# Moving the down-projection weights to other buffers at a stage boundary of a fused forward-and-backward kernel

## The chip, the cores and the metric

The kernel runs on one core of a Trainium2 chip. The metric is the device time of one execution in microseconds (us). The kernel before took 2054.99 us as the median of five runs (2052.01 to 2065.15). One further execution was taken by the hardware profiler.

The engines that appear below are PE (TensorE, the matrix unit; PEld is its weight load), DVE (VectorE), ACT (ScalarE), POOL (GpSimd) and SP (SyncE, which here only issues DMAs). SP, ACT and POOL each issue DMAs into a queue of their own; "SPq" in a profile line is the issue itself. An engine works through its own instructions in program order, so an instruction that waits holds back everything behind it on that engine.

## The reference

The program computes a block and all its gradients for a sequence of S = 2048 tokens, D = 1024 channels and F = 3584 hidden channels:

```
xn  = layernorm(x)
s   = xn * (longconv(shiftconv(k) * v) + ssm_D * shiftconv(k) * v)   # sequence mixing, by FFT
h   = (xn @ w_gate) * (xn @ w_up)                                    # [S, F]
g   = silu(h @ w_down)                                               # [S, D]
out = x + s * g
```

and then, for a given `grad_out`, the gradients for x, k, v, shift_k, ssm_k, ssm_D, w_gate, w_up and w_down. All inputs and outputs are bf16.

## The kernel before, in words

The work is laid out in stages for PE, and other engines' work is woven between them. Tokens come in 16 blocks of 128 (`b`), hidden channels in 14 slabs of 256 (`sl`) or 28 blocks of 128 (`fc`).

1. **Gate and up projection.** For each slab and each group of four token blocks, `gu_unit` does 32 matmuls (L556). ACT copies each PSUM result into `gut` (L558), and ACT stores `gut` to DRAM as `GUd`. DVE multiplies the halves into `hN`, and POOL stores that as `Hd`. A deferred closure `turn` transposes `hN` on PE (L570), ACT copies the result to `hT` (L571, two buffers) and POOL stores it as `HTd`. The forward convolution (PE, DVE, ACT) is pumped in between; its result goes out over POOL as `YFd`. The last two slabs (12 and 13) run together: first for the token blocks 0 to 7 (`hf = 0`), then for 8 to 15 (`hf = 1`).
2. **Down projection.** For each token block `b`, `bm_mm` (L967) does 28 x 2 matmuls with `w_down` into one PSUM tile `psbm` of three. The blocks go in pairs `bp`; the transposed `h` of a pair is `ht`, loaded from `HTd` (`load_ht`, two buffers). For the first pair it is `HT0`, in the two buffers U4 and U5. The first pair's matmuls run with `fc` outermost, four matmuls for each `fc`. After each block, `gate` loads four rows from DRAM (`x_t`, `do_t`, `xn_t`, `yf_t`), and ACT and DVE make the output and the gradients that flow back from the gate; they are stored by POOL as `DBMd`, `DYd` and `DXNAd`.
3. **Gradients of h, gate and up weights.** `dh_half` (L1091) and `dw_slab` (L1110), with the backward convolution pumped in between on DVE, PE, ACT and POOL.
4. **Gradient of the down weights** (L1209), then **gradient of x** (L1232).

**The buffers.** Eight tiles U0 to U7, of 1 MB each (128 partitions x 4096 bf16), live from the start. U0 to U3 hold the transposed normalised input `XNT` in stage 1, four token blocks each, so the last to read U0 and U1 are the matmuls of slab 13 in `hf = 0`, and the last to read U2 and U3 those of slab 13 in `hf = 1`. Four more, U8 to U11 (pool `ub`), and the `ht` buffers (pool `mh`) are allocated only after stage 1, in the memory that stage 1's pools (`fw`, `fg`: the slabs, `gut`, `hN`, `hT`) leave, so the first load into them waits until stage 1's last store of these has landed.

`WD[j]` are the seven 1 MB pieces of `w_down` that stage 2 reads, four `fc` each. Before, WD0 and WD1 are in U6 and U7 and are loaded before the last two slabs; WD2 and WD3 are in U2 and U3, WD4 to WD6 in U9, U10 and U8, and they are loaded after stage 1. `DBMT` (stage 2 and 3, transposed gradient of the gate) is in U0, U1, U4 and U5; `XN` (the normalised input for stage 3) in U7 to U10; `gu_in` cycles `GUd` pieces through U11, U6, U2, U3 and U12.

**The order.** The program text gives each instruction its place; a scheduler then orders each engine's instructions. It hoists loads: the eight gate rows of blocks 0 and 1 are written after the matmuls in the text, but stand in SP's order between the loads of WD2 and WD4. `tc.issue_after(x)` keeps what stands under it behind `x`. SP's order around the boundary, before:

```
WD0, WD1, HT0[0], HT0[1] rows 16-23, HT0[1] rows 24-27,
WD2 (U2), x_t do_t xn_t yf_t (block 0), WD3 (U3), x_t do_t xn_t yf_t (block 1),
WD4 (U9), WD5 (U10), WD6 (U8), ht of pair 1, ht of pair 2, ...
```

The loads under `ld` all have line L62 and the stores under `st` line L65, as each is issued by a helper.

Of the kernel before, what the change touches and what calls it, by code (L numbers as in the profile page):

```python
# [19 lines left out]
def build_kernel(  # L20
# [17 lines left out]
    DC = D // P  # L38
# [22 lines left out]
    def ld(out, in_):  # L61
        return nc.sync.dma_start(out=out, in_=in_)  # L62

    def st(out, in_):
        return nc.gpsimd.dma_start(out=out, in_=in_)  # L65
# [15 lines left out]
    def pool(name, bufs=1, side=None, space=None):  # L81
        kw = dict(name=name, bufs=bufs, reuse_waits="tile")
        if side:
            kw["side"] = side
        if space is not None:
            kw["space"] = space
        return tc.alloc_tile_pool(**kw)
# [109 lines left out]
    def tt(o, a, b, op):  # L197
        V.tensor_tensor(o, a, b, op)  # L198
# [261 lines left out]
    def u8(i, pat="p (a x) -> p a x", **kw):  # L460
        return U[i][:].rearrange(pat, **kw)
# [76 lines left out]
    def defer(fn):  # L538
        later.append([0, fn])

    def flush(age=0):

        for e in later:
            e[0] += 1
        while later and later[0][0] >= age:
            later.pop(0)[1]()
# [194 lines left out]
    def load_wd(j):  # L741
        return ld(WD[j], B_w_down[j * 512:(j + 1) * 512, :].rearrange("(c p) d -> p c d", p=P))

    def ht_rows(bp, f0, f1):
        j = (bp % 4) * 256
        return HTd[bp // 4][f0 // 24][f0 % 24 * P:(f0 % 24 + f1 - f0) * P, j:j + 256].rearrange("(c f) s -> f c s", f=P)


    WD = [u8(6, a=4), u8(7, a=4)]
    HT0 = [u8(4, a=16), u8(5, a=16)]  # L750
    with tc.issue_after(slab_ld.ins):
        load_wd(0)
# [2 lines left out]
    for hf in range(2):  # L755
        if hf == 1:
            flush()
            ld(HT0[1][:, 8:12], ht_rows(0, 24, 28))
        for sl in range(NSL - 2, NSL):
            for b0 in (8 * hf, 8 * hf + 4):  # L760
                gu_unit(sl, b0, 4, slabs[sl - NSL + 2], tick)
            if (hf, sl) == (0, NSL - 2):

                assert len(h_out) == 8
                ld(HT0[1][:, 0:8], ht_rows(0, 16, 24))
# [193 lines left out]
    bpump, bdrain = make_pump(conv_backward(), C_TOTAL)  # L959

    ddo = const.tile([P, 8], BF16, name="ddo")
    WD += [u8(j, a=4) for j in (2, 3, 9, 10, 8)]
    DBMT = [u8(q, a=DC) for q in (0, 1, 4, 5)]

    def bm_mm(ps, ht, i, fc):
        for dh in range(2):
            nc.tensor.matmul(ps[:, dh * 512:(dh + 1) * 512], ht(fc)[:, i * P:(i + 1) * P],  # L967
                             WD[fc // 4][:, fc % 4, dh * 512:(dh + 1) * 512], start=(fc == 0), stop=(fc == NF - 1))

    tr_name = ["tr"]  # L970

    def gate(b, ps):
        c, r = divmod(b, 8)
        ins = []
        for nm_, src in (("x_t", xq[:, c, r, :]), ("do_t", gout[:, c, r, :]), ("xn_t", XNd[:, b, :]), ("yf_t", YFd[:, b, :])):
            t = mi.tile([P, D], BF16, name=nm_)
            ld(t[:], src)
            ins.append(t[:])
        x_t, do_t, xn_t, yf_t = ins
        T = lambda nm_: mt.tile([P, D], BF16, name=nm_)[:]  # L980
        O = lambda nm_: mo.tile([P, D], BF16, name=nm_)[:]
        bm, sig, sgn, gg, so, dgg, ds_t = [T(n_) for n_ in ("bm", "sig", "sgn", "gg", "so", "dgg", "ds_t")]
        dbm, dy, dxa, o_t = [O(n_) for n_ in ("dbm", "dy", "dxa", "o_t")]
        nc.scalar.copy(out=bm, in_=ps[:])
        nc.scalar.activation(sig, bm, ACT.Sigmoid)
        nc.scalar.activation(sgn, bm, ACT.Sigmoid, scale=-1.0)
        tt(so, xn_t, yf_t, MUL)
        tt(dgg, do_t, so, MUL)
        tt(gg, bm, sig, MUL)
        tt(sgn, sgn, gg, MUL)  # L990
        tt(sig, sig, sgn, ADD)
        tt(dbm, dgg, sig, MUL)
        st(DBMd[b * P:(b + 1) * P, :], dbm)
        tt(ds_t, do_t, gg, MUL)
        tt(dy, ds_t, xn_t, MUL)
        st(DYd[:, :, b, :].rearrange("e u d -> u e d"), dy.rearrange("u (e d) -> u e d", e=8))
        tt(dxa, ds_t, yf_t, MUL)
        st(DXNAd[:, b, :], dxa)
        tt(o_t, so, gg, MUL)
        tt(o_t, o_t, x_t, ADD)  # L1000
        st(o_out[:, c, r, :], o_t)

        def turn():
            ps = ps_tr.tile([P, DC, P], BF16, name=tr_name[0])
            for dc in range(DC):
                nc.tensor.transpose(ps[:, dc, :], dbm[:, dc * P:(dc + 1) * P], ident[:])
            nc.scalar.copy(out=DBMT[b // 4][:, :, (b % 4) * P:(b % 4 + 1) * P], in_=ps[:])
        if b >= 12:
            defer(turn)
# [18 lines left out]
            ld(t, GUd[k // 2, k % 2])  # L1028
            DGU[k] = t

    for j in range(2, 7):
        wd_ld = load_wd(j)
    with tc.issue_after(wd_ld.ins):
        ht1 = load_ht(1)
# [4 lines left out]
    for i in range(2):  # L1039
        gate(i, pss[i])  # L1040
    for bp in range(1, 8):
        ht, ht_ld = load_ht(bp) if bp > 1 else ht1
        if bp in (3, 5, 7):
            q = (bp - 3) // 2
            with tc.issue_after(ht_ld.ins):
                nc.sync.dma_start_transpose(out=DBMT[q], in_=DBMd[512 * q:512 * q + 512, :])
        if bp == 6:
# [13 lines left out]

    XN = [u8(q, a=4) for q in (7, 8, 9, 10)]
    bg = pool("bg", 2, side="right")
    U.append(bg.tile([P, 4096], BF16, name="U12", bufs=1))
    ps_b = ps_tr = pool("ps_b", 3, space=PSUM)
# [7 lines left out]
    def btick(n):  # L1075
        bcnt[0] += n
        bpump((bcnt[0] - 10) / (BT - 10))

    def dh_half(k, wdt):
# [3 lines left out]
        for g in range(2):  # L1083
            bs = slice(4 * g, 4 * g + 4)
            dht = bg.tile([P, 4, SLW], BF16, name="dht", bufs=3)
            for e in range(2):
                ps = ps_b.tile([P, 512], F32, name="psb")
                for x in range(2):
                    b = 4 * g + 2 * e + x
                    for dc in range(DC):  # L1090
                        nc.tensor.matmul(ps[:, x * SLW:(x + 1) * SLW], DBMT[2 * hf + g][:, dc, (b % 4) * P:(b % 4 + 1) * P],  # L1091
                                         wdt[:, dc, :], start=(dc == 0), stop=(dc == DC - 1))
# [13 lines left out]
    def dw_slab(sl, dgus):  # L1106
        for dc in range(DC):
            ps = ps_b.tile([P, 512], F32, name="psb")
            for b in range(NB):
                nc.tensor.matmul(ps[:], XN[b // 4][:, b % 4, dc * P:(dc + 1) * P],  # L1110
                                 dgus[b // 8][:, b % 8].rearrange("p a f -> p (a f)"),
# [9 lines left out]
    def load_h(sl, home):  # L1121
        h = u8(home, "p (b f) -> p b f", b=NB)
        ld(h, Hd[sl])
        return h
# [6 lines left out]
    for q in range(4):  # L1131
        ld(XN[q], XNd[:, 4 * q:4 * q + 4, :])
    for k in (3, 4):
        gu_in(k)
    first = dh_half(0, wdt)
    DBM = [u8(q, a=4) for q in (0, 1, 4, 5)]
    HSL = (3, 11, 6)
    for sl in range(NSL):
        dgus = [first, dh_half(2 * sl + 1, wdts[sl])]
# [4 lines left out]
        else:  # L1144

            hs = {0: load_h(0, HSL[0])}
            for q in range(4):
                ld(DBM[q], DBMd[512 * q:512 * q + 512, :].rearrange("(b u) d -> u b d", u=P))
            hs[1] = load_h(1, HSL[1])
# [14 lines left out]
    def load_wgu(n, store):  # L1164
        a, j = pieces[n]
        WGU[n] = store
        nc.sync.dma_start_transpose(out=store, in_=(B_w_gate, B_w_up)[a][:, j * 512:(j + 1) * 512])

    def load_dgut(g, n):

        a, j = pieces[n]
        t = (gd2 if n < 4 else gd).tile([P, 4, 512], BF16, name=f"dgut{n}")
        nc.sync.dma_start_transpose(out=t[:], in_=DGd[j, a, 512 * g:512 * g + 512, :])
        return t
# [3 lines left out]
    for k in range(NSL):  # L1178
        if 0 < k and k + 1 < NSL:
            hs[k + 1] = load_h(k + 1, HSL[(k + 1) % 3])  # L1180
        if k == 0:
            hs[2] = load_h(2, HSL[2])
        with tc.issue_after(wst.ins) if k > 0 else nullcontext():
            if k in (1, 2, 3, 4, 5):
                load_wgu(k - 1, u8((7, 8, 9, 10, 2)[k - 1], a=4))
            if k in (6, 7, 8, 9):
                ts.append(load_dgut(0, k - 6))
        if k == 11:

            bdrain()  # L1190
            tip.release()
            gw = pool("gw", 1)
            gd = pool("gd", 1)
            for i in range(2):
                load_wgu(5 + i, gw.tile([P, 4, D], BF16, name=f"W{i}")[:])
            ts += [load_dgut(0, n) for n in range(4, 7)]
        if k == 12:
            load_wgu(7, u8(6, a=4))
            ts.append(load_dgut(0, 7))
        if k == 13:  # L1200
            load_wgu(8, u8(3, a=4))
            ts.append(load_dgut(0, 8))
        h = hs.pop(k)
        for f in range(2):
            wbs = wo.tile([P, D], BF16, name="wbs")[:]
            for dh in range(2):
                ps = ps_b.tile([P, 512], F32, name="psb")
                for b in range(NB):
                    nc.tensor.matmul(ps[:], h[:, b, f * P:(f + 1) * P], DBM[b // 4][:, b % 4, dh * 512:(dh + 1) * 512],  # L1209
                                     start=(b == 0), stop=(b == NB - 1))  # L1210
                nc.scalar.copy(out=wbs[:, dh * 512:(dh + 1) * 512], in_=ps[:])  # L1211
                btick(2)
            f0 = k * SLW + f * P
            wst = ld(o_dwd[f0:f0 + P, :], wbs)
# [50 lines left out]
            V.scalar_tensor_tensor(dx_t[:, cl], dxn[:, cl], RSTD[:, b:b + 1], dout_t[:, cl], op0=MUL, op1=ADD)  # L1265
            (st if parts == 1 else ld)(o_dx[:, c, r, cl], dx_t[:, cl])

    for i, j in enumerate((11, 0, 1, 4, 5)):
        load_wgu(9 + i, u8(j, a=4))
        ts.append(load_dgut(0, 9 + i))  # L1270
    for g in range(4):
# [88 lines left out]
```

## Time and profile before

| what | value |
|---|---|
| median of five runs | 2054.99 us (2052.01, 2052.61, 2054.99, 2063.32, 2065.15) |
| the profiled execution, device time | 2053.47 us |
| its span, first to last instruction | 2051.7 us, so 1.8 us lie around the span |
| PE busy | 1970.5 us, 96% of the span |
| DVE busy | 1485.3 us, 72% |
| ACT busy | 607.3 us, 30% |
| POOL busy | 343.7 us, 17% |
| DMA moved | 454.43 MB, mean 221 GB/s |
| stage 2, PE (L967) | from 572.1 to 774.4 us |

A line of the timeline reads: start in us, duration in us, engine, source line, operation, output <- inputs, shape, how many instructions were merged, and in brackets how long the engine had been idle before and what ended that. "PE busy" counts matmuls from issue to modelled end, so it says little about how fast the matmuls run; the distance between their starts does. PEclk is the clock that PE was granted, 1.00 being full. A line of the waits gives who waited, for whom, for how long in all, how many times, and the longest.

### The profile page before, as it was taken

How to read it: one execution, taken by the hardware profiler on the slowest of the kernel's cores; microseconds unless marked ns; L12 is line 12 of the kernel's file. 1: busy time of each engine (PE TensorE's matmuls, PEld its weight loads, DVE VectorE, ACT ScalarE, POOL GpSimd, SP SyncE). 2: the span in 40 equal slices, each digit the busy share in tenths (PEclk: the TensorE clock that was granted, in tenths of full speed). 3: DMA queues.
4: the chain of work that ended last, by engine and by line, in shares of the span. 5: the costliest groups of instructions: out<-in, count | busy, mean ns of one | idle time of the engine just before them, and what ended most of it. 6: DMA issues, size and time to landing. Idle time of an engine off the chain costs nothing.

```text
span 2051.7 us, 28854 instructions
## 1 busy us (share of the span) xinstructions
PE 1970.5 (96%) x11530; PEld 1056.2 (51%) x11530; DVE 1485.3 (72%) x2007; ACT 607.3 (30%) x956; POOL 343.7 (17%) x499
## 2 busy tenths in 40 slices
PE   6999999999989998999899889999999999999998
PEld 3455555555534445666566556555444444444443
DVE  7789999999826654888799999998978024444343
ACT  4644444445422223232222222222122101111112
POOL 4222222221112221000112211211111100110100
PEclk9999999999999999999999999999999999999999
DMA  9686766558499989675878688865996979393921
GB/s 300 226 281 218 247 211 237 195 195 277 171 306 303 273 273 317 209 220 164 273 247 262 223 229 242 263 219 197 253 233 174 241 186 213 115 215 93 235 69 57
DMA packets 468711, 454.43 MB, mean 221 GB/s; under 512 B 249456, under 2 KB 393624, under 8 KB 454624
## 3 DMA queue, kind: packets, MB, share of 16 engines
q1 hardware_dynamic: 324240, 190.08, 36.1%
q0 software_dynamic: 45200, 189.08, 27.3%
q10 hardware_dynamic: 99136, 73.42, 11.4%
q8 instruction: 90, 1.47, 0.3%
q14 instruction: 45, 0.37, 0.1%
HBM read 208.15 MB, written 194.02 MB: 196 GB/s over the span
## 4 chain that ended last, share of the span: by engine, by line
PE 60%; DVE 16%; issue 14%; DMA 5%; POOL 3%; ACT 1%; ACTq 0%; POOLq 0%; DVEq 0%; SPq 0%
PE psx L1232 19%; PE psb L1110 10%; PE psb L1209 9%; PE psbm L967 9%; DVE W L198 5%; PE psg L556 4%; DVE m L198 4%; PE psb L1091 4%; DVE HX L198 1%; DVE U L198 1%; DMA dyl<-DYd 1%; DVE KX L198 1%; POOL HTd L65 1%; PE psdk L943 1%; DVE B L242 1%
## 5 line engine op out<-in xcount | busy, mean ns | idle before, releaser
L556 PE MATMUL psg<-wslab,U 128*128 128x512 bf16 x1792 | 419.0, 385 | 8.0 <-DMA wslab<-in_B_w_gate_dram 3.1
L1110 PE MATMUL psb<-U,U 128*128 128x512 bf16 x1792 | 399.3, 382 | 10.5 <-ACT dht L1093 6.5
L1232 PE MATMUL psx<-U,dgut 128*128 128x512 bf16 x1536 | 335.7, 379 | 0.0
L1110 PEld LDWEIGHTS <-U 128*128 128x128 bf16 x1792 | 176.1, 98 | 215.3 <-issue 16.8
L1232 PEld LDWEIGHTS <-dgut 128*128 128x128 bf16 x1792 | 173.9, 98 | 211.0 <-issue 3.6
L556 PEld LDWEIGHTS <-U 128*128 128x128 bf16 x1792 | 174.8, 99 | 197.8 <-issue 16.9
L1091 PE MATMUL psb<-wdt,U 128*128 128x256 bf16 x1792 | 204.0, 274 | 10.1 <-ACT dht L1093 8.9
L558 ACT CAST gut<-psg 128x512 bf16<-128x512 f32 x224 | 131.3, 587 | 230.6 <-PE psg L556 219.5
L1209 PE MATMUL psb<-U,U 128*128 128x512 bf16 x896 | 195.8, 379 | 0.0
L1091 PEld LDWEIGHTS <-U 128*128 128x128 bf16 x1792 | 175.8, 98 | 33.9 <-issue 10.7
L967 PE MATMUL psbm<-U,ht 128*128 128x512 bf16 x784 | 169.9, 379 | 0.0
L1114 ACT CAST wb<-psb 128x512 bf16<-128x512 f32 x112 | 65.6, 586 | 313.5 <-PE psb L1110 217.5
L198 DVE TENSOR_TENSOR W<-W 128x1024 f32<-128x1024 f32 (+1 forms) x144 | 142.6, 1008 | 2.8
L1209 PEld LDWEIGHTS <-U 128*128 128x128 bf16 x896 | 87.1, 98 | 102.4
L198 DVE TENSOR_TENSOR m<-A,B 128x1024 bf16<-128x1024 bf16 (+1 forms) x160 | 116.5, 791 | 29.7 <-issue 21.1
L198 DVE TENSOR_TENSOR dka<-dkh,Wbc 128x1024 bf16<-128x1024 bf16 x16 | 11.1, 692 | 165.0 <-DMA dkh<-DKSHd 165.0
L967 PEld LDWEIGHTS <-ht 128*128 128x128 bf16 x784 | 76.6, 98 | 91.8
L1255 ACT ACTIVATE dx_t<-dxn 128x1024 bf16<-128x1024 f32 (+1 forms) x17 | 17.1, 1007 | 341.1 <-DVE dxn L198 287.1
L1093 ACT CAST dht<-psb 128x512 bf16<-128x512 f32 x112 | 65.0, 587 | 156.4 <-PE psb L1091 109.8
L198 DVE TENSOR_TENSOR U<-U,dht 128x2048 bf16<-128x2048 bf16 x56 | 70.2, 1254 | 25.1 <-ACT dht L1093 25.1
L198 DVE TENSOR_TENSOR W<-W,psP 128x512 f32<-128x512 f32 x128 | 80.4, 678 | 8.6 <-ACT W L228 6.7
L1211 ACT CAST wbs<-psb 128x512 bf16<-128x512 f32 x56 | 32.8, 586 | 159.5 <-PE psb L1209 145.3
(233 smaller groups left out, 2339.9 us busy)
## 6 DMA issues: line engine op xcount, KB each, us to landing
U<-GUd SPq DMA_DIRECT2D x28, 1024.0 KB, 7.5
DGd<-U ACTq DMA_DIRECT2D x56, 512.0 KB, 6.0
GUd<-gut ACTq DMA_DIRECT2D x54, 512.0 KB, 4.5
A<-DYFd POOLq DMA_DIRECT2D x16, 1024.0 KB, 5.5
U<-Hd SPq DMA_DIRECT2D x15, 1024.0 KB, 6.0
out_dram<-wb ACTq DMA_DIRECT2D x224, 64.0 KB, 3.7
Hd<-hN POOLq DMA_DIRECT2D x54, 256.0 KB, 3.5
HTd<-hT POOLq DMA_DIRECT2D x54, 256.0 KB, 3.7
```

Source lines behind the costliest of these rows:

```text
L65: return nc.gpsimd.dma_start(out=out, in_=in_)
L198: V.tensor_tensor(o, a, b, op)
L556: gu_mm[0] = nc.tensor.matmul(ps[:], XNT[q][:, dc, qi * P:(qi + 1) * P], w[:, dc].rearrange("p a f -> p (a f)"), start=(dc == 0), stop=(dc ...
L558: nc.scalar.copy(out=gut[:, i].rearrange("p a f -> p (a f)"), in_=ps[:])
L967: nc.tensor.matmul(ps[:, dh * 512:(dh + 1) * 512], ht(fc)[:, i * P:(i + 1) * P], WD[fc // 4][:, fc % 4, dh * 512:(dh + 1) * 512], start=(f ...
L1091: nc.tensor.matmul(ps[:, x * SLW:(x + 1) * SLW], DBMT[2 * hf + g][:, dc, (b % 4) * P:(b % 4 + 1) * P], wdt[:, dc, :], start=(dc == 0), sto ...
L1093: nc.scalar.copy(out=dht[:, 2 * e:2 * e + 2].rearrange("p b f -> p (b f)"), in_=ps[:])
L1110: nc.tensor.matmul(ps[:], XN[b // 4][:, b % 4, dc * P:(dc + 1) * P], dgus[b // 8][:, b % 8].rearrange("p a f -> p (a f)"), start=(b == 0), ...
L1114: nc.scalar.copy(out=wb[:].rearrange("p a f -> p (a f)"), in_=ps[:])
L1209: nc.tensor.matmul(ps[:], h[:, b, f * P:(f + 1) * P], DBM[b // 4][:, b % 4, dh * 512:(dh + 1) * 512], start=(b == 0), stop=(b == NB - 1))
L1211: nc.scalar.copy(out=wbs[:, dh * 512:(dh + 1) * 512], in_=ps[:])
L1232: nc.tensor.matmul(ps[:, dh * 512:(dh + 1) * 512], t[n][:, f, i * P:(i + 1) * P], WGU[n][:, f, dh * 512:(dh + 1) * 512], start=(n == 0 and ...
```

## The change

The changed kernel gives five of the seven pieces of `w_down` other buffers, loads two of them earlier in the text, and puts the gate rows of the first two blocks behind the last of them.

- WD2 and WD3 go to U0 and U1, WD4 and WD5 to U2 and U3, and WD6 to U9. WD2 and WD3 are loaded in the text at the start of `hf = 1`, ahead of the last HT0 rows.
- `DBMT` and later `DBM` go to U10, U8, U4 and U5 in place of U0, U1, U4 and U5. `XN` goes to U7, U0, U1 and U9 in place of U7 to U10. The homes of the transposed gate and up weights in stage 4 follow.
- The loads of the gate rows of blocks 0 and 1 stand under `issue_after(wd_ld.ins)`, where `wd_ld` is the load of WD6.

```diff
-    WD = [u8(6, a=4), u8(7, a=4)]
+    WD = [u8(j, a=4) for j in (6, 7, 0, 1)]
...
         if hf == 1:
             flush()
+            load_wd(2)
+            wd_ld = load_wd(3)
             ld(HT0[1][:, 8:12], ht_rows(0, 24, 28))
...
-    WD += [u8(j, a=4) for j in (2, 3, 9, 10, 8)]
-    DBMT = [u8(q, a=DC) for q in (0, 1, 4, 5)]
+    WD += [u8(j, a=4) for j in (2, 3, 9)]
+    DBMT = [u8(q, a=DC) for q in (10, 8, 4, 5)]
...
             t = mi.tile([P, D], BF16, name=nm_)
-            ld(t[:], src)
+            with tc.issue_after(wd_ld.ins) if b < 2 else nullcontext():
+                ld(t[:], src)
...
-    for j in range(2, 7):
+    for j in range(4, 7):
         wd_ld = load_wd(j)
...
-    XN = [u8(q, a=4) for q in (7, 8, 9, 10)]
+    XN = [u8(q, a=4) for q in (7, 0, 1, 9)]
...
-    DBM = [u8(q, a=4) for q in (0, 1, 4, 5)]
+    DBM = [u8(q, a=4) for q in (10, 8, 4, 5)]
...
-                load_wgu(k - 1, u8((7, 8, 9, 10, 2)[k - 1], a=4))
+                load_wgu(k - 1, u8((7, 0, 1, 9, 2)[k - 1], a=4))
...
-    for i, j in enumerate((11, 0, 1, 4, 5)):
+    for i, j in enumerate((11, 10, 8, 4, 5)):
```

The order in which PE, DVE, ACT and POOL run their instructions is the same in both kernels. SP's order around the boundary, after:

```
WD0, WD1, HT0[0], HT0[1] rows 16-23,
WD2 (U0), WD3 (U1), HT0[1] rows 24-27, WD4 (U2), WD5 (U3), WD6 (U9),
ht of pair 1, x_t do_t xn_t yf_t (block 0), x_t do_t xn_t yf_t (block 1), ht of pair 2, ...
```

At the end of stage 2, SP's order was GU1, XN, GU2, XN, XN, XN, GU3, GU4 (1 MB each) and becomes GU1, XN, XN, GU2, XN, XN, GU3, GU4. Nothing else in SP's order differs but the names of the buffers.

## The prediction

> **What bounds the kernel now.** First the page's first part: PE is busy for 1970.5 of 2051.7 us, so only a stage in which PE stands still can give time. Then PE's waits in the stretch of stage 2's first pair, and its timeline there.
>
> ```profile
> PE 1970.5 (96%) x11530; PEld 1056.2 (51%) x11530; DVE 1485.3 (72%) x2007; ACT 607.3 (30%) x956; POOL 343.7 (17%) x499
> ```
>
> ```profile
> PE psbm L967 <- DMA U<-in_B_w_down_dram: 5.7, 2, 5.4
> ```
>
> ```profile
> 572.09 10.52 PE L967 MATMUL psbm<-U,U 128*128 128x512 bf16 x48
> 582.92 3.61 PE L967 MATMUL psbm<-U,U 128*128 128x512 bf16 x16 [0.31 <-DMA U<-in_B_w_down_dram]
> 591.89 12.00 PE L967 MATMUL psbm<-U,U 128*128 128x512 bf16 x48 [5.35 <-DMA U<-in_B_w_down_dram]
> 603.72 16.57 PE L967 MATMUL psbm<-U,ht 128*128 128x512 bf16 x76
> ```
>
> PE stops twice for `w_down`: before its fourth piece (WD3, after 48 matmuls) and its fifth (WD4, after 64). The first row gives the pace: (10.52 - 0.38) / 47 = 0.216 us from start to start. At that pace the 112 matmuls of the pair end at 572.09 + 112 x 0.2158 = 596.26, and the next pair begins at 603.72. So 7.46 us are lost: 0.47 at WD3, 5.52 at WD4, and 1.47 in the row after it, whose 48 matmuls took 11.83 us where 10.36 would do.
>
> Why WD4 is late is read in the chain of work, SP's timeline and ACT's.
>
> ```profile
> 580.43 5.70 DMA HTd<-hT
> ...
> 586.35 5.50 DMA U<-in_B_w_down_dram
> ```
>
> ```profile
> 562.77 0.37 SPq L62 DMA_DIRECT2D U<-in_B_w_down_dram  x1
> 563.28 0.41 SPq L62 DMA_DIRECT2D x_t<-in_A_q_dram  x1
> 563.74 0.43 SPq L62 DMA_DIRECT2D do_t<-in_grad_out_dram  x1
> 564.21 0.66 SPq L62 DMA_DIRECT2D xn_t<-XNd  x1
> 574.56 0.33 SPq L62 DMA_DIRECT2D yf_t<-YFd  x1
> 574.99 0.42 SPq L62 DMA_DIRECT2D U<-in_B_w_down_dram  x1
> ...
> 586.35 1.48 SPq L62 DMA_DIRECT2D U<-in_B_w_down_dram  x3
> 587.87 18.50 SPq L62 DMA_DIRECT2D ht<-HTd  x4
> ```
>
> ```profile
> 579.13 1.01 ACT L571 COPY hT<-tr 128x1024 bf16<-128x1024 bf16 x1 [7.54 <-DMA HTd<-hT]
> ```
>
> WD3's buffer is free at 570.1 (the last gate-and-up matmul), but SP sits on `yf_t`, which waits until the store of `YFd` (issued at 564.02) has landed, and issues WD3 at 574.99. WD4 to WD6 wait for the last `HTd` store: the third `hT` copy needs a buffer whose store landed at 579.1; so that store was issued at 580.43, landed at 586.13, and SP issued WD4 at 586.35.
>
> **What the Trainium skill says.** "DMA: Bandwidth & Descriptors", section "Anatomy of one DMA — SWDGE (gpsimd) path": a wait is made by the issuing engine before it dispatches, so one waiting load holds all behind it. The trace agrees: `yf_t` held WD3 for 4.5 us. The same page, "Queues, rings and completion order": the 16 DMA engines take turns between the queues that have work, and serve one queue in order. The trace fits: with WD2 and three gate rows on SP's queue, `YFd` needed 10.5 us, and 8.4 us at 517 us with fewer loads. "TensorE: Matmul & The Clock Gate", "What's actually happening": about 3.4 us of idle halve PE's clock until it has been busy as long. The trace agrees: after the stop of 5.35 us the weight loads are 0.43 us apart for seven matmuls, then 0.22 us; 7 x 0.21 us is the 1.47 us above.
>
> **The change, part by part.**
>
> *WD2 and WD3 earlier.* The gate-and-up stores of `GUd` at 528.62 and 535.97 close the units that last read U0 and U1. So WD2 goes out at about 528 and WD3 at 535 to 536 and land by about 546; they are needed at 572.09 + 32 x 0.2158 = 579.0 and 582.4. The stop of 0.47 us goes. The price is 2 MB more among the stores there. A `gut` buffer is needed again by the second unit after it: the store of 528.62 by 537.5, that of 535.97 by 545.8. Each has 8.9 and 9.8 us; such a store took 4.5 us here as median and 9.9 us in the crowded stretch at 563. So 0 to 1 us of PE; I take 0.2. The last HT0 rows now stand behind WD3 (539.71 before); needed at 592.8, they cost nothing.
>
> *WD4 and WD5 in U2 and U3.* They go out when their buffers are free, at 562.8 and 570.1, with no gate row between. With 5 to 8 us to landing they are there by 571 and 578; needed at 572.09 + 64 x 0.2158 = 585.9 and at 589.4.
>
> *WD6 in U9* still waits for the last `HTd` store. Before, that lands at 586.13. Now 0.75 MB of gate rows before 570 are gone, and WD5 comes 5 us sooner. I bound the issue of WD6, t0, by 580 (`hT` copied at 575, store issued at 576.3, 3.3 us to landing as at 541 to 560) and by 586.35 (nothing gained), and take 583. WD6 lands 5.5 us later, at 585.5 to 591.9; PE needs it at 572.09 + 96 x 0.2158 = 592.8. In time at both ends: the 5.52 us and the 1.47 us go.
>
> *`ht` of pair 1* follows WD6 on SP's queue; its first 1.5 MB are needed at 596.3. The rate: WD4 to WD6 and this load, 4.5 MB, went from 586.35 to 602.8 (14.9 us to landing, issued at 587.87), 3.65 us a MB. So 2.5 MB land at t0 + 9.1 us, up to 10.6 with the other queues: 589 to 597. That is 0 to 0.7 us of PE; I take 0.2.
>
> *Gate rows.* 2 MB behind 2.75 MB: block 0's land at about t0 + 13.7, at 594 to 600, block 1's by 604. Before, DVE began the gate's `gg` 3.4 us after the pair's end (603.49 to 606.90); now it could at 599.7 and may start 2 us late, since `so` and `dgg` (0.69 us each) stand ahead of it on DVE. What hides this: DVE is busy for 104 of the 170 us from 604 to 774, and PE feels it only when block 4 wants block 1's `psbm` tile, freed when ACT has copied it, which waits for block 0's `gg`: at 596.3 + 24.2 = 620.4. The rows would have to land after about 617.
>
> *End of stage 2.* XN's second and third MB come from U0 and U1 (free sooner than U9 and U8), GU2 waits for U2's WD4, 3.5 us later than WD2. The queue is at 0.9 to 1.0 of the DMA's time there, so 8 MB take as long; first use of GU2 is 15 us after the stage. I take 0, from -3.3 (a load no longer waits for the last `fc`) to +3.
>
> *Other homes.* The rest of the lists follow the same lifetimes one for one; no engine's order changes. 0.
>
> Sum: -7.46 + 0.2 + 0.2 = about -7.1 us. Stage 2 then runs without waits (PE 170.00 of 170.00 us from 604 to 774), and what follows starts from its end, so it all moves up. On its own time: span 2051.7 - 7.1 = 2044.6, execution 2053.47 - 7.1 = 2046.4. The runs' median lies 1.5 us above the profiled execution: 2047.9, that is 0.35% less. A measurement of this kernel tells about 0.5%, or 10.3 us, from no change.
>
> **The rivals.**
>
> *A second gain at the junction (2043).* From 774 to 823 PE is busy for only 42.09 of 49 us and its clock is at 0.93: 8 MB of loads crowd out small stores, and ACT hangs for 5.57 us in one DMA issue. If XN's earlier release clears that queue 3.3 us sooner, each wait shortens by as much, some 3 to 6 us on top: 2042 to 2045. For it: XN loads wait from 771.02 to about 775.3 in SP's order. Against: the DMA engines are full meanwhile.
>
> *The gain is eaten later (2053).* From 1000 to 1150 DVE is busy for 144.89 of 150 us and the chain runs over it and over loads such as the 14.36 us on `B<-HFd`. If that stretch is timed by something that does not move, half or all of the 7 us stay there: 2051 to 2055. Against: the convolution begins with `DYd`, which moves with stage 2.
>
> *Slower (2066): WD6 becomes the wait.* SP's queue now holds `ht` and all gate rows behind WD6. PE's stop begins when t0 passes 585.7 and eats the gain at 593.1; the kernel is 10 us slower from t0 = 603 on. For it: WD5 and the `HTd` stores now share the time from 570 to 577. Against: 17 us later than before with less queued. Price at t0 = 604: 2055 + 11 = 2066.
>
> *The change does nothing (2055).* If WD6's store decided all; excluded, as WD6 is needed 6.9 us later than WD4 was (592.8, not 585.9).
>
> **How the numbers follow.** Main case 0.58, own range 2044.5 to 2050.5; junction 0.20; eaten later, with nothing gained, 0.13; slower 0.09. Two of the five runs before lie 8 and 10 us above their median, so a median may shift by some us. The range 2041 to 2056 leaves out the slower case and the far tail of the junction. Faster by over 0.5% (below 2044.7): the junction case and a little of the main one's spread, 0.26; slower by over 0.5%: 0.09; within: 0.65.
>
> **What would show it.** Right: no wait of L967 for `w_down`; the pair's 112 matmuls in about 24.2 us at clock 1.00; first `ht` matmul near 596.3 to 597; WD3 issued near 536, WD6 near 583; stage 2 ends at 767; distances between later stages as before. Wrong: a wait of L967 for WD6 or `ht`; ACT waiting for `GUd` or `HTd` stores at 535 to 550; the stretch from 774 to 823 or from 1000 to 1150 changed by more than 3 us.

## The result and the profile after

The changed kernel takes 2049.01 us (median of 44 runs, 2043.29 to 2060.99). The kernel before took 2056.16 us beside it (median of 79 runs, 2047.84 to 2065.18). The ratio is 0.9967, with a 95% interval of 0.9959 to 0.9976: 0.33% faster. That is less than the 0.5% that a measurement of this kernel tells from no change, but with so many runs the interval leaves 1 out. The forecast was 2047.9 us.

The profiled execution took 2049.98 us (span 2048.2 us), against 2053.47 us (span 2051.7 us) before. First the page's first part of the kernel after.

```profile
PE 1969.1 (96%) x11530; PEld 1055.8 (52%) x11530; DVE 1484.9 (72%) x2007; ACT 606.6 (30%) x956; POOL 341.3 (17%) x499
```

The shares tell nothing: PE was "busy" for 96% in both. The stretch of stage 2's first pair tells more. These are the busy times in the same 32 us, of before and then of after. The columns are the window, its length, busy time and number of instructions of PE, PEld, DVE, ACT and POOL, PE's granted clock, the DMA share and GB/s.

```profile
572.00:604.00 32.00, 26.34 (x119) 11.59 (x117) 1.38 (x2) 1.52 (x2) 1.71 (x3) 0.95 0.94 308
```

```profile
572.00:604.00 32.00, 32.00 (x152) 14.52 (x150) 5.99 (x10) 7.57 (x8) 3.04 (x5) 1.00 1.00 302
```

In the same time PE issued 152 matmuls where it issued 119, at full clock; the DMA engines moved no more (302 GB/s against 308). So the transfers did not become faster; what was brought first is what changed. PE's timeline of the kernel after, where that of before had four rows and two stops:

```profile
572.00 24.34 PE L969 MATMUL psbm<-U,U 128*128 128x512 bf16 x112
596.17 16.14 PE L969 MATMUL psbm<-U,ht 128*128 128x512 bf16 x74
```

The 112 matmuls of the pair run as one row, with no wait for any DMA, and the next pair begins 24.17 us after the first: 7.46 us less than before (31.63). SP's timeline of the kernel after shows why; then WD6 alone, from a narrower look at the same queue; then ACT's third `hT` copy and POOL's store of it.

```profile
527.96 7.72 SPq L62 DMA_DIRECT2D U<-in_B_w_down_dram  x2
543.83 0.37 SPq L62 DMA_DIRECT2D U<-HTd  x1
562.70 17.95 SPq L62 DMA_DIRECT2D U<-in_B_w_down_dram  x3
580.70 6.83 SPq L62 DMA_DIRECT2D ht<-HTd  x2
587.58 0.86 SPq L62 DMA_DIRECT2D x_t<-in_A_q_dram  x1
...
589.49 0.37 SPq L62 DMA_DIRECT2D yf_t<-YFd  x1
```

```profile
580.27 0.37 SPq L62 DMA_DIRECT2D U<-in_B_w_down_dram  x1
```

```profile
574.46 1.01 ACT L571 COPY hT<-tr 128x1024 bf16<-128x1024 bf16 x1 [2.95 <-DMA HTd<-hT]
```

```profile
575.76 0.73 POOL L65 DMA_DIRECT2D HTd<-hT  x1 [2.87 <-ACT hT L571]
```

WD2 and WD3 go out from 527.96, WD4 and WD5 from 562.70, and only the third load of that row, WD6, waits for stores. The last `HTd` store is issued at 575.76, 4.67 us earlier than before (580.43), because the copy ahead of it waited 2.95 us and not 7.54 us for an older store. It landed 4.3 us later, at about 580.06, and WD6 went out at 580.27; PE needs it at 572.00 + 20.7 = 592.7. `ht`, issued at 580.70, landed 10.7 us later, at 591.4; PE needs it at 596.17.

The span shrank by 3.5 us and not by 7.5. This table has the starts of the stages on PE in the two profiled executions (first matmul of the first pair, of the second pair, of L1091 or L1094, of L1209 or L1212, of L1232 or L1235), and the length of each stretch.

| stretch | before: start | length | after: start | length |
|---|---|---|---|---|
| first pair of stage 2 | 572.09 | 31.63 | 572.00 | 24.17 |
| rest of stage 2 | 603.72 | 171.9 | 596.17 | 171.9 |
| stage 3 | 775.58 | 659.7 | 768.04 | 658.3 |
| stage 4 | 1435.3 | 203.0 | 1426.3 | 203.1 |
| stage 5, to the last matmul | 1638.3 | 403.8 | 1629.4 | 409.2 |

The gain is there, with 1.4 us more, when stage 5 begins. Then 5.4 us go in stage 5 of this one execution: a stop of PE and the slower clock that follows it. In the kernel after, PE's timeline and DVE's at that place:

```profile
1837.78 12.21 PE L1235 MATMUL psx<-U,dgut 128*128 128x512 bf16 x48 [3.70 <-DVE dxn L198]
```

```profile
1831.66 0.69 DVE L198 TENSOR_TENSOR dka<-dkh,Wbc 128x1024 bf16<-128x1024 bf16 x1 [13.19 <-DMA dkh<-DKSHd]
```

DVE stood 13.19 us for `dkh`, then made seven `dka` and `dkp` before the `dxn` that frees PE's PSUM tile. That load took 8.9 us from issue to landing; before, 5.2 us. Of the twelve profiled executions in this study (before, after and ten more), this stop is in eight, 1.5 to 6.3 us long: after (3.7), e2 (3.8), e3 (5.7), e4 (1.5), e6 (4.7), e7 (6.3), e8 (1.6), e10 (2.6, in two). It is not in before, e1, e5 and e9. e7 keeps all the old buffers, e6 all but the order of WD4 to WD6, e10 is the kernel after once more, e1 has the new homes and no stop; three of the four profiles with the old homes have it, and five of the eight with the new ones. So it comes and goes from one execution to the next and is not of the change; the medians, 7.15 us apart, do not show it either. A second, smaller stop in stage 5 is in e6 and e7 alone, both with the old homes of the gate and up weights: 1.8 and 2.1 us in all, for loads of `w_up`. The other two profiles with the old homes (before, e2) lack it, and so do all eight with the new ones; that is too few to call it an effect of the homes. Why `dkh` lands late in some executions was not found.

### The profile page after: what moved, and what is told of

Read it like the earlier page. It is cut to its first block, busy times and chain, and to the rows that moved or that the text cites. A ratio compares the mean times of both kernels' runs of the same rounds, so it can differ in the third digit from the quotient of the medians.

```text
span 2048.2 us, 28857 instructions
## 1 busy us (share of the span) xinstructions
PE 1969.1 (96%) x11530; PEld 1055.8 (52%) x11530; DVE 1484.9 (72%) x2007; ACT 606.6 (30%) x956; POOL 341.3 (17%) x499
## 4 chain that ended last, share of the span: by engine, by line
PE 61%; DVE 21%; issue 9%; DMA 5%; POOL 1%; ACT 1%; ACTq 0%; SPq 0%; DVEq 0%; POOLq 0%
PE psx L1235 18%; PE psbm L969 9%; PE psb L1212 9%; PE psb L1113 9%; DVE W L198 6%; PE psg L556 6%; DVE m L198 6%; PE psb L1094 4%; DVE HX L198 2%; DVE U L198 1%; DMA B<-HFd 1%; DVE KX L198 1%; DMA dyl<-DYd 1%; PE psY L403 1%; DVE B L198 1%
## 5 line engine op out<-in xcount | busy, mean ns | idle before, releaser
L1235 PE MATMUL psx<-U,dgut 128*128 128x512 bf16 x1536 | 337.4, 380 | 3.7 <-DVE dxn L198 3.7
L1235 PEld LDWEIGHTS <-dgut 128*128 128x128 bf16 x1792 | 174.4, 98 | 215.9 <-issue 9.6
L1094 PE MATMUL psb<-wdt,U 128*128 128x256 bf16 x1792 | 204.0, 274 | 9.3 <-ACT dht L1096 8.2
L1212 PE MATMUL psb<-U,U 128*128 128x512 bf16 x896 | 195.8, 379 | 0.0
L1094 PEld LDWEIGHTS <-U 128*128 128x128 bf16 x1792 | 175.8, 98 | 33.2 <-issue 10.0
L198 DVE TENSOR_TENSOR dka<-dkh,Wbc 128x1024 bf16<-128x1024 bf16 x16 | 11.1, 691 | 181.5 <-DMA dkh<-DKSHd 181.5
L1212 PEld LDWEIGHTS <-U 128*128 128x128 bf16 x896 | 87.1, 98 | 102.4
```

The lines of the kernel that those rows point to most:

```text
L1235: nc.tensor.matmul(ps[:, dh * 512:(dh + 1) * 512], t[n][:, f, i * P:(i + 1) * P], WGU[n][:, f, dh * 512:(dh + 1) * 512], start=(n == 0 and ...
```

## The experiments

The theory: the whole gain is PE's stop in the first pair, us for us; it went because WD4 and WD5 no longer stand behind the last `HTd` store, and because that store lands sooner without gate rows in its way. The rivals: only one half of the change matters; the next load in the queue (WD6, `ht`) is about to become the wait; and there is a second gain, or a loss, at the junction of stages 2 and 3.

### The new homes alone

The gate rows stay where the scheduler puts them.

```diff
-            with tc.issue_after(wd_ld.ins) if b < 2 else nullcontext():
-                ld(t[:], src)
+            ld(t[:], src)
```

> The changed kernel with its gate rows left free again: the weights keep their new homes and early loads, the rows of blocks 0 and 1 go out as early as SP's order gives. My theory: the time is lost only where PE stops for w_down in the first pair. SP then sits on yf_t until about 574.5, WD5 goes out near 575 and lands near 581 (needed at 589.4), the last HTd store lands near 586 as before, WD6 lands near 591.8 (needed at 592.8), ht of pair 1 near 597.4 (needed at 596.2). So PE stops about 1 us and 6 us of the gain stay: ratio to before 0.997 (0.9963 to 0.9978). Rival, the rows make the gain: with the rows back, WD6 stops PE for 4 us or more and the ratio is 0.999 or above.

Measured: 2050.57 us, ratio 0.9973 (0.9961 to 0.9986). SP's timeline and PE's of this kernel:

```profile
573.24 0.33 SPq L62 DMA_DIRECT2D yf_t<-YFd  x1
573.67 0.69 SPq L62 DMA_DIRECT2D U<-in_B_w_down_dram  x1
...
585.06 0.38 SPq L62 DMA_DIRECT2D U<-in_B_w_down_dram  x1
```

```profile
571.49 24.34 PE L969 MATMUL psbm<-U,U 128*128 128x512 bf16 x112
596.13 8.16 PE L969 MATMUL psbm<-U,ht 128*128 128x512 bf16 x37 [0.30 <-DMA ht<-HTd]
```

`yf_t` holds the load behind it on SP as before, but now that is WD5 (573.67), not WD3, and it is needed at 571.49 + 17.3 = 588.8. (The Trainium skill, "DMA: Bandwidth & Descriptors", section "Anatomy of one DMA — SWDGE (gpsimd) path", has a wait made by the issuing engine before it dispatches; here SP stood for 8.2 us, from the end of the `xn_t` issue at 565.04 to 573.24, and the delay falls on whichever load comes next.) WD6 goes out at 585.06, 13.6 us after the pair's first matmul, nearly as late as WD4 before (14.3), and still comes in time. `ht` is 0.30 us late, where 1 us was expected. The pair takes 24.64 us: the new homes alone take 7.0 of the 7.46 us away.

### The gate rows alone

The kernel before, with only the two lines that put the gate rows behind the last `w_down` load.

```diff
-            ld(t[:], src)
+            with tc.issue_after(wd_ld.ins) if b < 2 else nullcontext():
+                ld(t[:], src)
```

> The kernel before with one edit: the gate rows of blocks 0 and 1 stand behind the last weight load; all homes as before, so WD4 to WD6 all wait for the last HTd store. My theory: with the rows gone from 563 to 577 that store lands near 580 as in the changed kernel, WD4 lands near 585.7 (needed at 585.9), WD5 near 589.3 (589.4), WD6 near 593 (592.8), ht near 596.6 (596.2): all just in time, PE stops 0 to 1.5 us in all, and the ratio to before is 0.997 (0.9963 to 0.9978). Rival, the homes make the gain: the HTd store lands at 586 and PE stops about 5 us at WD4, ratio 0.999 to 1.000.

Measured: 2050.27 us, 0.9974 (0.9960 to 0.9987). PE's timeline of this kernel, and POOL's issue of the last `HTd` store:

```profile
571.00 13.98 PE L967 MATMUL psbm<-U,U 128*128 128x512 bf16 x64
585.92 10.52 PE L967 MATMUL psbm<-U,U 128*128 128x512 bf16 x48 [0.94 <-DMA U<-in_B_w_down_dram]
596.99 7.30 PE L967 MATMUL psbm<-U,ht 128*128 128x512 bf16 x33 [0.56 <-DMA ht<-HTd]
```

```profile
575.28 0.73 POOL L65 DMA_DIRECT2D HTd<-hT  x1 [3.40 <-ACT hT L571]
```

WD4 is still behind the last `HTd` store, but that store was issued at 575.28, for want of gate rows in its way; PE stops for 0.94 us at WD4, after 64 matmuls as before, and 0.56 us at `ht`. The pair takes 25.99 us, 5.6 us less than before. Both runs came out as expected. Each half alone does most of it (7.0 and 5.6 of 7.46 us in the pair): the halves overlap and do not add up. The rival that only one half matters falls; the ratios, with their intervals, would not tell the three kernels apart.

### Three more megabytes ahead of WD6, and behind it

Two kernels load 3 MB more (rows 0 to 511 of `w_down`, three times, into U10, U8 and U11, which nothing reads before they are written again), to shift what follows. First ahead of WD6:

```diff
-    for j in range(4, 7):
+    for j in (4, 5):
         wd_ld = load_wd(j)
+    for i in (10, 8, 11):
+        with tc.issue_after(wd_ld.ins):
+            wd_ld = ld(u8(i, a=4), B_w_down[0:512, :].rearrange("(c p) d -> p c d", p=P))
+    with tc.issue_after(wd_ld.ins):
+        wd_ld = load_wd(6)
```

> The changed kernel with 3 MB of loads that nobody reads (three copies of the first piece of w_down, into U10, U8 and U11) put on SP's queue between WD5 and WD6. At 3.65 us a MB WD6 lands near 580.3 + 14.6 = 595 (needed at 592.8) and ht of pair 1 near 580.3 + 20.1 = 600.4 or later (needed at 596.2). My theory, what PE stops for in the first pair goes one to one into the end: PE stops about 2 us at WD6 and 3 us more at ht, with up to 1.5 us of slow clock, and the kernel is 4 to 6.5 us slower than the changed one: ratio to before 0.9988 to 1.0000. Rival, the gain comes from the end of stage 2 and the junction, not from this stop: no slower than the changed kernel, ratio 0.9967.

Measured: 2048.45 us, 0.9968 (0.9954 to 0.9982): no slower than the kernel after. The expectation failed. The windows of this kernel and of the kernel after, with the columns as above:

```profile
572.00:582.00 10.00, 10.00 (x53) 4.81 (x53) 0.00 (x0) 1.01 (x1) 2.01 (x3) 1.00 0.99 359
```

```profile
572.00:582.00 10.00, 10.00 (x50) 4.56 (x48) 0.00 (x0) 1.01 (x1) 1.62 (x3) 1.00 0.71 255
```

In the kernel after, the DMA share is only 0.71 in these 10 us, in most of which WD6 waits for stores; here it is 0.99. SP's timeline of this kernel, in that stretch:

```profile
571.28 0.81 SPq L62 DMA_DIRECT2D U<-in_B_w_down_dram  x1
577.33 1.13 SPq L62 DMA_DIRECT2D U<-in_B_w_down_dram  x2
```

The extra loads went out at 571.28 and 577.33, before the last `HTd` store had landed, and filled that gap. U10, U8 and U11 do not wait for this store. WD6, in U9, does: it went out at 582.61, 0.1 us after the store issued at 576.21 had landed (6.3 us). From this I take it that of the four only U9 lies in memory that the store reads. I had taken all four to wait alike, as they come from one pool, in the description ahead of the prediction and in the prediction. `ht` landed at about 596.7, 24.3 us after the pair's start and 4.9 us later than in the kernel after (19.4), just in time. So this run did not reach the point that it was made to test. The next one did: the same loads behind WD6.

```diff
     for j in range(4, 7):
         wd_ld = load_wd(j)
+    for i in (10, 8, 11):
+        with tc.issue_after(wd_ld.ins):
+            wd_ld = ld(u8(i, a=4), B_w_down[0:512, :].rearrange("(c p) d -> p c d", p=P))
```

> The changed kernel with the 3 MB of loads that nobody reads (U10, U8, U11) behind WD6 instead of ahead of it. In the run with them ahead, they went out before the last HTd store had landed and filled time in which SP's queue was empty; behind WD6 they can't. ht of pair 1 landed at 591.4 in the changed kernel (issued at 580.7, 10.7 us), so with 3 MB at 3.65 us it lands near 602 (needed at 596.2). My theory, a stop in the first pair goes one to one into the end: PE stops about 6 us before the first ht matmul, with 1 to 1.5 us of slow clock, and the gain is gone: ratio to before 0.9990 to 1.0010. Rival, later stages take such a stop up: ratio below 0.998.

Measured: 2053.29 us, 0.9993 (0.9977 to 1.0009). PE's waits and its timeline in this kernel:

```profile
PE psbm L969 <- DMA ht<-HTd: 4.1, 1, 4.1
```

```profile
571.21 24.34 PE L969 MATMUL psbm<-U,U 128*128 128x512 bf16 x112
599.70 4.67 PE L969 MATMUL psbm<-U,ht 128*128 128x512 bf16 x13 [4.15 <-DMA ht<-HTd]
```

The only edit against the kernel after is the 3 MB between WD6 and `ht`; the gate rows behind `ht` move with it. The stop costs 28.49 - 24.17 = 4.3 us in the pair and 173.6 - 171.9 = 1.7 us of slow clock in the rest of stage 2, 6.0 us in all, and the ratio loses 0.26%, that is 5 us, give or take 4 us by the two intervals. So within that uncertainty a stop at this place, with its slow clock, is paid us for us, and the gain is the stop; the rival that later stages take it up (ratio below 0.998) does not fit. The stop came out at 4.15 us and not 6, because the 3 MB delayed `ht` by 9.0 us (28.4 against 19.4 us after the pair's start) and not by 3 x 3.65 = 10.9. Of those 9.0 us the first 4.8 are the reserve that the kernel after has.

### WD4 to WD6 in another order of buffers

The kernel before, with WD4 to WD6 in U10, U8 and U9 in place of U9, U10 and U8: with what e3 taught, only the last of them would wait for the store.

```diff
-    WD += [u8(j, a=4) for j in (2, 3, 9, 10, 8)]
+    WD += [u8(j, a=4) for j in (2, 3, 10, 8, 9)]
```

> The kernel before with WD4 and WD6 exchanged: WD4 to WD6 go to U10, U8 and U9 in place of U9, U10 and U8; nothing else. My theory: only U9 lies in memory that the last HTd store reads from, U10 and U8 do not; so WD4 and WD5 go out right behind block 1's gate rows, near 578, and land near 584 to 588 (needed at 585.9 and 589.4), WD6 near 591.8 (592.8), ht near 597 (596.2): PE stops 0 to 2.5 us in all in place of 5.7, ratio to before 0.9965 to 0.9983. Rival, all three wait for the last HTd store whichever comes first: PE stops over 5 us at WD4 as before, ratio 0.9993 to 1.0007.

Measured: 2055.06 us, 0.9992 (0.9976 to 1.0008). The expected gain did not come. PE's timeline of this kernel and SP's:

```profile
580.62 3.61 PE L967 MATMUL psbm<-U,U 128*128 128x512 bf16 x16 [0.35 <-DMA U<-in_B_w_down_dram]
586.62 12.21 PE L967 MATMUL psbm<-U,U 128*128 128x512 bf16 x48 [2.39 <-DMA U<-in_B_w_down_dram]
```

```profile
575.98 8.16 SPq L62 DMA_DIRECT2D U<-in_B_w_down_dram  x3
```

WD4 does go out at 575.98, 6.2 us after the pair's first matmul where before it was 14.3, and WD6, now in U9, at 583.77, 0.2 us after the last `HTd` store (issued at 577.54) had landed. So the part about U9 holds, and the rival that all three wait for this store falls. But WD4 stands behind WD3 and four gate rows, 2 MB on the same queue, and needed 10.6 us to land, where before it needed 5.5: a stop of 2.39 us is left, with 1.7 us of slow clock after it. The two stops, 2.7 us, are a little over the 2.5 us expected at most. The pair takes 28.92 us, 2.7 us less than before, too little for this timing to show. An early issue is not an early landing where other loads stand in front.

### A second gain at the junction?

At the junction PE is busy for 42.35 of 49 us in the kernel after (from 767.0) and for 42.15 in the kernel before (from 774.5): the change did next to nothing there. To see whether a gain was to be had, GU3 and GU4 (2 MB) were put behind the third transposed load of stage 3, in the kernel after (e4, and once more as e8) and in the kernel before (e7). `wdt_ld[0]` holds the latest transposed load.

```diff
-    for k in (3, 4):
-        gu_in(k)
...
     for sl in range(NSL):
         dgus = [first, dh_half(2 * sl + 1, wdts[sl])]
...
+        if sl == 0:
+            with tc.issue_after(wdt_ld[0].ins):
+                for k in (3, 4):
+                    gu_in(k)
```

> The changed kernel with two of the eight 1 MB loads at the junction of stages 2 and 3 (GU3 and GU4, first used by the fourth and fifth dh_half) put on SP's queue behind the third transposed load of the down weights, at about 790 in place of 767. From 766.6 to 815.6 the changed kernel has PE busy for 42.24 of 49 us at clock 0.97. If the crowded queue is what holds PE there (the rival of a second gain at the junction), dyx lands some us sooner, ACT's hang in the DGd issues (2.81 and 8.98 us) shrinks, and the time falls 2 to 6 us below the changed kernel: ratio to before 0.994 to 0.9957. If the small-packet DGd stores hold ACT by themselves, the two loads only move into them: ratio 0.9962 to 0.9980, PE busy there 42 of 49 us as now.

> The kernel before with GU3 and GU4 put behind the third transposed load of the down weights, as in the run with the changed kernel. My theory: the junction's loss is the same in both kernels, whatever the homes; so the stop at WD4 stays (5 to 6 us) and the junction loses 4 to 5 us less: ratio to before 0.9965 to 0.9985. Rival, the junction's gain needs the new order of the XN loads: ratio 0.9993 to 1.0007.

> The changed kernel with GU3 and GU4 late once more, as its first timing rested on few runs: ratio to before 0.9935 to 0.9955 if the junction's 4 to 5 us come on top of the change's 7, 0.9967 if they do not.

Measured: e4 2044.23 us, 0.9943 (0.9921 to 0.9965), of six runs only; e8, the same kernel, 2046.16 us, 0.9961 (0.9947 to 0.9975); e7 2055.40 us, 1.0003 (0.9986 to 1.0020). The windows of the junction and of what follows it, of before and then of e7, each from a point 1.1 us ahead of stage 3's first matmul:

```profile
774.50:823.50 49.00, 42.15 (x320) 28.75 (x320) 25.63 (x37) 15.12 (x24) 5.73 (x10) 0.93 0.99 292
823.50:874.50 51.00, 50.93 (x407) 31.66 (x406) 42.18 (x68) 14.67 (x27) 4.25 (x8) 1.00 0.71 222
```

```profile
771.40:820.40 49.00, 46.91 (x386) 32.06 (x385) 26.82 (x38) 17.39 (x28) 5.73 (x10) 1.00 0.92 297
820.40:871.40 51.00, 46.30 (x343) 28.68 (x344) 42.08 (x69) 13.21 (x25) 4.25 (x8) 0.97 0.71 224
```

PE's timeline of e7 in the second window:

```profile
825.03 0.61 PE L215 MATMUL psP<-dyx,TF 128*128 128x256 bf16 x2 [4.92 <-DVE W L198]
```

e7's expected ratio, 0.9965 to 0.9985, failed. The measured one is the rival's, but not for the rival's reason, as the junction did gain without the new order of the `XN` loads: it gets 66 matmuls more in its 49 us. The next 51 us get 64 fewer: PE runs ahead into the first transform of the backward convolution, on which DVE works without a break from 810.7 to 827, and waits for `W`. That work of DVE begins 39.3 us after the start of the first window, and 38.7 us in before: it did not move. Stage 3 takes 660.3 us against 659.7. That is what the rival of the prediction missed: in e7 PE's 6.9 idle us at the junction are slack, since DVE sets the time of what comes behind. In e8 the same two stretches have 61 matmuls more and 56 fewer than in the kernel after, with the same wait, of 4.1 us. There stage 3 is perhaps a little shorter: 652.8, 658.0 and 655.8 us in the three profiles with the new homes and the late loads (e4, e8, e9), 657.6 to 660.6 in the five without. The ratio of e8 lies between its two expected ones, and e4's, in the range expected of a gain, was lower than that of either later run with these loads (e8, and e9 below); whether the late GU loads are worth 0 or some 3 us on top of the change stays open.

### A better version?

A last pair of runs has the late GU loads together with an earlier `dkh` load against the stop in stage 5, beside the kernel after on the same chip.

```diff
-            kh = ew.tile([P, 11, P], BF16, name="kh")
-            cld_k(kh[:], c, ds)
...
+            kh = ew.tile([P, 11, P], BF16, name="kh")
+            cld_k(kh[:], c, ds)
```

> The changed kernel with GU3 and GU4 late, and in the last stage the load of dkh (which DVE waits for) put ahead of the load of kh (which only PE reads). In six of ten profiles PE stops for 1.5 to 6.3 us in the last stage, as DVE holds a PSUM tile's dxn behind a dka that waits for dkh; dkh is issued 0.54 us after kh and lands behind its 0.35 MB, so it should land 0.5 to 1.5 us sooner. If that near miss decides, the stop shrinks or goes and the ratio to before is 0.9935 to 0.9955; if it is the transposed loads that hold dkh, 0.9955 to 0.9970 as without this edit.

> The changed kernel once more, beside the one with two further edits, for a comparison on one chip and for one more look at the last stage: ratio to before 0.9960 to 0.9975; first pair of stage 2 in 24.2 us with no wait for weights; the last stage 403 to 412 us long, by chance.

(The count of profiles with the stop in the first text is off by one: it was seven of ten then.)

Measured: e9 2046.67 us, 0.9966 (0.9954 to 0.9978); the kernel after (e10) 2048.26 us, 0.9973 (0.9960 to 0.9986). The stop in stage 5 is absent in e9's profile, and stage 5 takes 403.6 us there, about as in before (403.8); but four of the twelve profiles lack it, so one profile proves nothing. The ratio is in the range expected without any help from the `dkh` edit, the intervals overlap, and e9 could not be told from the kernel after. In e10 the first pair takes 24.17 us again, to the hundredth.

## Why the prediction was right

- **The stop and its size.** Forecast: 7.46 us of PE go, less 0.2 and 0.2. Measured: the pair is 7.46 us shorter. The medians are 7.15 us apart; the ratio gives 4.9 to 8.4 us. e5 showed the exchange to be one to one within some 4 us. The forecast point was 1.1 us too low, and the median before had been taken as 2054.99 us, of five runs, where 79 runs give 2056.16: about the same shift. The mechanism is shown; that 7.1 and 7.15 agree to less than 0.1 us is luck, as the interval is 3.5 us wide.
- **WD2 and WD3 among the stores (0.2 us).** They went out at 528 and 535, as forecast. The two `GUd` stores there took 7.1 us to land (median) where 4.5 us were assumed, but under the 8.9 us that they have, and ACT waited for no store from 528 to 560. Cost: 0.
- **t0, the issue of WD6 (580 to 586.35, taken 583).** Measured 580.27, at the lower end: the third `hT` copy waited 2.95 us. That WD4 to WD6 all wait for the last `HTd` store was read too widely. In the kernel before, the load of U9 stood first and held the other two behind it, and in the changed kernel WD6 is the one load in U9, so the forecast did not suffer; e3 and e6 showed it. e1 gives the upper end, 585.06 with the gate rows left in place, and WD6 was in time there too, so the choice between the bounds decided nothing.
- **`ht` of pair 1 (0.2 us).** Landed at t0 + 11.1, a little beyond the t0 + 9.1 to 10.6 that was worked out; as t0 was early it had 4.8 us in hand. At the t0 of 583 that was taken, the same 11.1 us would still have left some 2 us, an estimate from these figures. Cost: 0. Here was the smallest margin: e1 (0.3 us late), e2 (0.6) and e5 (4.15) all stop there.
- **Gate rows (0 to 2 us late, hidden).** DVE's timeline of the kernel after:

```profile
596.05 0.69 DVE L198 TENSOR_TENSOR so<-xn_t,yf_t 128x1024 bf16<-128x1024 bf16 x1 [24.74 <-DMA yf_t<-YFd]
...
599.36 0.69 DVE L198 TENSOR_TENSOR gg<-bm,sig 128x1024 bf16<-128x1024 bf16 x1 [1.89 <-ACT sig L988]
```

  The last row of block 0 landed at about 596.0, t0 + 15.7 (t0 + 13.7 forecast). `so` started at once, and `gg` at 599.36, 3.4 us after ACT began the copy of `bm`: as long as before. What released `gg` is ACT, not a load. No delay at all.
- **The junction (0, from -3.3 to +3).** PE's busy time in its 49 us is 42.35 against 42.15; stage 3 is 1.4 us shorter, where the twelve profiles spread from 652.8 to 662.3 us. The choice of 0 held.
- **Later stages as before.** True of the rest of stage 2, of stage 3 within its spread and of stage 4. Not of stage 5 in this profile (5.4 us longer), which the forecast did not have: a stop that comes in some executions of old and new homes alike.
- **The rivals.** "A second gain at the junction": the change brought none, and in e7 PE gives back behind it what it gains there. "Eaten later": excluded by the medians and by the starts of the stages up to stage 5. "WD6 becomes the wait": its mechanism is real, but one load further on; e5 makes `ht` the wait and takes the gain away, with 3 MB more on SP's queue. "The change does nothing": refuted, as the interval ends at 0.9976.

What stays open: why `dkh` lands late in some executions of stage 5, and what the late GU loads are worth. To take away U9's wait for the store while all else stays was not tried.

## What to carry to other kernels

Where loads share a queue at a stage boundary, write down for each load when its consumer needs it and what it waits for before it goes out. A load that waits for old stores should be the one needed last, and loads that nobody needs yet should stand behind those that somebody does; either half was nearly enough here, so two remedies for one wait should not be added up. Price a stop of the bounding engine by its own length and, where it is long enough, the slow clock behind it (here behind stops of 2.4 us and more, not behind those of 1.8 us and less), and idle time beside a second busy engine at nothing until the next stretch is looked at.

## What the runs showed that was not expected

- Buffers of one pool do not wait alike. U10, U8 and U11 took loads at 571 and 577 us, U9 only after the last `HTd` store (582.61 in the same run, 580.27 in the kernel after). SP waited for a `GUd` store ahead of the load of U8, and for `Hd` and `HTd` stores ahead of that of U9: what counts, it seems, is which old buffer lay in the same memory.
- PE's clock halves after shorter stops than the Trainium skill lets one think. "TensorE: Matmul & The Clock Gate", section "What's actually happening", names an idle window of about 3.4 us. In e6 a stop of 2.39 us was followed by a granted clock of 0.50 to 0.67 for 4 us, and 48 matmuls took 1.7 us more than at full clock. That is as much as after 4.15 us (e5, 1.7) and 5.35 us (before, 1.5), and less than after 4.85 us (e7, 2.4). One of these 4 us in e6, with the columns as above; the granted clock is the 0.50:

```profile
587.60:588.60 1.00, 1.00 (x4) 0.44 (x3) 0.00 (x0) 0.00 (x0) 0.00 (x0) 0.50 1.02 379
```

  After 0.94 us (e2), and after 1.54, 1.63 and 1.82 us in stage 5 (e4, e8, e10), there was no such loss: the row of 48 matmuls took 10.52 us each time. The measurement decides: in this one execution a stop of 2.4 us cost 4.1.
- 3 MB more on the queue delayed `ht` by 4.9 us when they could use the gap ahead of WD6, and by 9.0 us when they stood behind it.
